# Six batches of normalised A transposed by a DMA in place of TensorE, with another token order and other scheduling constants

## The chip, the cores and the metric

The kernel runs on one core of one Trainium2 chip. The metric is device time in microseconds (us): the median of several executions, of which there are three for the kernel before. Beside them one execution was profiled; its span, from the first to the last instruction, and its own time are given below. The engines are named as in the profile: PE is TensorE, PEld its weight loads, DVE is VectorE, ACT is ScalarE, POOL is GpSimd, SP is SyncE (which only issues DMAs here).

## The reference

A Nyström attention, followed by a multiplicative feed-forward. There are 8 batches, 8 heads, 576 tokens, 64 features a head, and 32 landmarks, each the mean of 18 successive tokens.

```python
q_lm = q.reshape(B, H, m, S // m, D).mean(axis=3)      # and k_lm alike
A  = sm(q, k_lm)          # softmax(scale * q k_lm^T): 576 x 32 a head
Bm = sm(q_lm, k_lm)       # 32 x 32
C  = sm(q_lm, k)          # 32 x 576
Z  = Bm^T / (norms);  six times  Z = 2 Z - Z Bm Z
attn = A @ Z @ C @ v
x = attn as 4608 tokens x 512 features
out = (((x @ w1) * (x @ w2)) @ w3) @ w_out             # inner width 1024, out 4608 x 512
```

## The kernel before

Four heads make a quad; two quads are a batch (quads 2b and 2b + 1 are batch b). A quad's work runs through all engines: GpSimd's DMA queue loads q and k (as fp16, tokens with heads and landmarks on the partitions), DVE transposes 32 x 32 blocks of them into Tq and Tk, POOL, ACT and DVE make the landmark means and place them in lmT, PE makes the scores. Two batches are a group. A group's Bm and Z are iterated together in 32 x 32 matmuls (tile xz), Z, C and v make W (tile wT), and W is multiplied by w1 and w2 (u_mm, 64 x 32 tiles of PE) into u, 128 x 1024 a quad and matrix. So the tokens come in only at the end: the dense part computes A^T against u.

The A path of one quad, in order: `a_mm` (scores of 512 tokens in four blocks of 128, L691), `a_rest` (the last 64 tokens of both quads, odd quads only), `a_max`, `a_sub` (DVE), `a_exp` (ACT), `a_sum` (DVE), `a_norm` (POOL, L744; writes ah, of which there are two), `a_trans` (PE, L753; four transposes 128 x 128 to PSUM, a fifth in odd quads for the rest), `a_copy` (ACT, L763, and L766 for the rest; writes aT and puts tokens into their order). In a block of `a_mm`, a row of PSUM is a token (r, l): r counts within a landmark's 18 tokens, l is the landmark; block i holds four r and all 32 l. `a_copy` turns that to (l, r).

The dense part: for each batch, three thirds th of 192 tokens and eight blocks j of 128 inner columns, a task d (`d1_mm`: four matmuls of 192 columns, both products x @ w1 and x @ w2 in one PSUM bank), e (`d1_a`, L1097: ACT takes one product out to asb), f (`d1_b`, L1103: DVE multiplies the two into ab). Then, for each of 36 tiles t of 128 tokens, g (`d2_mm`: two halves of four matmuls of 512 columns, ab against w34 = w3 @ w_out), h (`d2_a`, L1129: ACT takes it out, four buffers osb) and st (`d2_store`, L1144, from SP; the last two tiles use ACT's queue as well). Tile 35 is made in two halves of 256 columns. w34 itself is computed in the first 80 us (`w34_mm`, in two fp16 parts).

The order of all instructions is not written by hand. Every piece of work is a task with an engine, an assumed duration, what it depends on, what buffers it takes and frees, and a priority (a time; the smaller goes first). `Plan.run` simulates the engines and the DMA queues with these assumptions and gives the order in which the tasks are emitted; each engine then executes its instructions strictly in that order. Among the tasks of PE that could start within 0.05 us of the first, the one of least priority wins; a task that keeps the present mode of PE (full array, or a kind of tiles) has a bonus, MP for the full mode and MT for the tiled ones. Where the priorities come from: `dense(b) = T0 + PER * b` is a batch's dense time; task d of batch b, third th, block j has `dense(b) + PER * (8 * th + j) / 24`, tile t has `T0 + PER * (128 * t + 128) / S + GO`; `att(n)` gives the quads, `lane(g)` the groups. PSUM has six banks that these tasks share (ring "P") and a wide one for the scores.

Of the kernel before, what the change touches and what calls it, by code (L numbers as in the profile page):

```python
# [15 lines left out]
S = 576  # L16
# [3 lines left out]
GRP = S // M  # L20
# [2 lines left out]
DF = 1024  # L23
HALF = 288
MP = 1.8
MT = 6.0
MY = 0.0
GR = int(2.0)
THIRD = 192
# [184 lines left out]
def kernel(  # L214
# [11 lines left out]
    nc = tc.nc  # L226
    P = Plan()
# [62 lines left out]
    def at(key, i=0):  # L290
        return P.slot[key][i]
# [3 lines left out]
    def mm(out_, lhsT, rhs, start=True, stop=True, pos=None):  # L295
        nc.tensor.matmul(out_, lhsT, rhs, start=start, stop=stop,  # L296
                         **({} if pos is None else {"tile_position": pos}))
# [4 lines left out]
    NS = [2 * len(bs) for bs in GROUPS]  # L302


    T0 = 65.0
    PER = 20.0

    def dense(b):
        return T0 + PER * b
# [1 line left out]
    def att(n):  # L311
        bs = GROUPS[GOF[n // 2][0]]
        k = n - 2 * bs[0] - 2 * len(bs) + 4
        first = dense(bs[0]) - 55.0 + 8.0 * k
        if n < 4:
            first = 10.0 + 6.5 * n
        return max(12.0 + 6.0 * n, first)

    def lane(g):
# [6 lines left out]
    LQ = int(1.0)  # L326
    NT = 2 * int(2.0)
    NE = int(2.0)
    L0 = 3.0
    UO = 2.0  # L330
    GO = 10.0


    def const_a():
# [134 lines left out]
        return fn  # L469

    W1 = 2.0
    JS = int(4.0)
    JH = 3.0
    PWL = [(), (3,), (1, 4), (1, 3, 5), (1, 3, 5, 7)][int(2.0)]
    PEB = int(2.0)
# [209 lines left out]
    def a_bank(n):  # L685
        return psS.rearrange("p a x -> p (a x)") if n % 2 else bank(at(f"pA{n}"))

    def a_cols(n):
        return 640 if n % 2 else 512

    def a_mm(n):  # L691
        def fn():
            T, lm, ps, o = Tqs[at(f"Tq{n}")], lmTs[at(f"lmT{n}")], a_bank(n), 4 if n % 2 else 2
            for i in range(4):
                for e in range(2):
                    mm(ps[:, 128 * i:128 * i + 128], T[:, o + 4 * i:o + 4 * i + 4, :, e], lm[:, 4:8, :, e],
                       start=(e == 0), stop=(e == 1))
        return fn

# [41 lines left out]
    def a_norm(n):  # L741
        def fn():
            g = a_cols(n) // M
            nc.gpsimd.tensor_tensor(  # L744
                out=ahs[at(f"ah{n}")][:, 0:g, :], in0=eas[at(f"ea{n}")][:, 0:g, :],
                in1=tinies[at(f"ta{n}")][:, 0:g].unsqueeze(2).to_broadcast([128, g, M]), op=ALU.mult)
        return fn

    def a_trans(n):
        def fn():  # L750
            ps = bank(at(f"pT{n}")).bitcast(FP16)
            for i in range(a_cols(n) // 128):
                nc.tensor.transpose(  # L753
                    out=ps[:, 128 * i:128 * i + 128],
                    in_=ahs[at(f"ah{n}")][:, 4 * i:4 * i + 4, :].rearrange("p g m -> p (g m)"),
                    identity=ident16[:, :])
        return fn

    def a_copy(n):
        def fn():  # L760
            b, qd = divmod(n, 2)
            ps, t = bank(at(f"pT{n}")).bitcast(FP16), aTs[at(f"aT{b}")]
            nc.scalar.copy(out=t[:, qd, 0:512].rearrange("p (i l r) -> p i l r", i=4, r=4),  # L763
                           in_=ps[:, 0:512].rearrange("p (i r l) -> p i l r", i=4, r=4))
            if qd:
                nc.scalar.copy(out=t[:, :, 512:S].rearrange("p a (l r) -> p a l r", r=2),  # L766
                               in_=ps[:, 512:640].rearrange("p (a r l) -> p a l r", a=2, r=2))
        return fn

    def quad_tasks(n):  # L770
# [56 lines left out]
        else:  # L827
# [7 lines left out]
            rel=[f"pA{n}"], prio=p + 0.7)  # L835
        add(f"ae{n}", "ACT", 0.63 if qd else 0.53, a_exp(n), deps=[f"as{n}"], prio=p + 3.0)
        add(f"au{n}", "DVE", 1.03 if qd else 0.9, a_sum(n), deps=[f"ae{n}"], prio=p + 4.0)
        add(f"an{n}", "POOL", 1.3 if qd else 1.05, a_norm(n), deps=[f"au{n}"], acq=[("ah", f"ah{n}", 1, 1)],
            rel=[f"ea{n}", f"ta{n}"], prio=p + 5.0)
        add(f"tA{n}", "PE", 0.36 if qd else 0.29, a_trans(n), deps=[f"an{n}", "cd"],  # L840
            acq=[("P", f"pT{n}", 1, 1)], rel=[f"ah{n}"], prio=p + 9.0, mode="full")
        add(f"aT{n}", "ACT", 0.65 if qd else 0.48, a_copy(n), deps=[f"tA{n}"] + ([f"aT{n - 1}"] if qd else []),
            acq=[] if qd else [("aT", f"aT{b}", 1, 24)], rel=[f"pT{n}"], prio=p + 9.5)


    def cv_mm(b):
# [286 lines left out]
    def d2_store(t, f0=0, f1=DM, part=None, eng=nc.sync):  # L1133
        def fn():
            k = 0
            o_sb = osb[at(f"os{t}")]
            p0 = 0
            while p0 < 128:
                b, x = divmod(128 * t + p0, S)
                i, u = divmod(x, 128)  # L1140
                n = 4 if i < 4 else 2
                w = min(128 - p0, 32 * n - u)
                if part in (None, k):
                    eng.dma_start(  # L1144
                        out=out[S * b:S * b + S, :].rearrange("(l r) f -> l r f", r=GRP)[
                            u // n:(u + w) // n, 4 * i:4 * i + n, f0:f1],
                        in_=o_sb[p0:p0 + w, f0:f1])
                p0, k = p0 + w, k + 1
        return fn

# [3 lines left out]
    def dense_tasks():  # L1154
        for k in range(3 * B):
            b, th = divmod(k, 3)
            for j in range(8):
                p = dense(b) + PER * (8 * th + j) / 24.0
                deps = [f"aT{2 * b}", f"aT{2 * b + 1}"]
                deps += [f"uo{b}{wi}{j // 4}{qd}" for wi in range(2) for qd in range(2)]  # L1160
                add(f"d{b}{j}{th}", "PE", 0.33, d1_mm(b, j, th), deps=deps + ["wo7"],
                    acq=[("P", f"pD{b}{j}{th}", 1, 1)],
                    rel=[f"u{b}0", f"u{b}1", f"aT{b}"], prio=p, mode="full")
                add(f"e{b}{j}{th}", "ACT", 0.21, d1_a(b, j, th), deps=[f"d{b}{j}{th}"],
                    acq=[("asb", f"as{b}{j}{th}", 1, 1)], prio=p)
                acq = [(f"ab{k % NCH}", f"ab{k}", 1, 2 * len(chunk_tiles(k)))] if j == 0 else []
                add(f"f{b}{j}{th}", "DVE", 0.27, d1_b(b, j, th),
                    deps=[f"e{b}{j}{th}"] + ([f"f{b}0{th}"] if j else []), acq=acq,
                    rel=[f"as{b}{j}{th}", f"pD{b}{j}{th}"], prio=p)
        for t in range(36):  # L1170
            ks = [k for k in range(3 * B) if t in chunk_tiles(k)]
            p = T0 + PER * (128 * t + 128) / S + GO
            fs = [f"f{k // 3}{j}{k % 3}" for k in ks for j in range(8)]
            if t == 35:
                for h in range(2):
                    add(f"g{t}_{h}", "PE", 0.86, d2_last(t, h), deps=fs + ([f"g{t}_0"] if h else []),
                        acq=[("P", f"pE{t}{h}", 1, 1)], rel=[f"ab{k}" for k in ks], prio=p + 0.9 * h, mode="full")
                    add(f"h{t}_{h}", "ACT", 0.3, d2_lasta(t, h), deps=[f"g{t}_{h}"],
                        acq=[] if h else [("osb", f"os{t}", 1, 4)], rel=[f"pE{t}{h}"], prio=p + 2.0)
                    for i, (eng, q) in enumerate((("SP", nc.sync), ("ACT", nc.scalar))):  # L1180
                        add(f"st{t}_{h}{i}", eng, 0.55, d2_store(t, 256 * h, 256 * h + 256, i, q),
                            deps=[f"h{t}_{h}"], rel=[f"os{t}"], prio=p + 2.0, move=0.25, lat=1.5, share=2.0)
                continue
            for h in range(2):
                add(f"g{t}_{h}", "PE", 0.86, d2_mm(t, h), deps=fs + ([f"g{t}_0"] if h else []),
                    acq=[] if h else [("P", f"pE{t}", 1, 1)], rel=[f"ab{k}" for k in ks], prio=p + 0.9 * h,
                    mode="full")
            add(f"h{t}", "ACT", 0.48, d2_a(t), deps=[f"g{t}_1"],
                acq=[("osb", f"os{t}", 1, 2 if t == 34 else 1)], rel=[f"pE{t}"], prio=p + 2.0)
            if t == 34:  # L1190
                for i, (eng, q) in enumerate((("SP", nc.sync), ("ACT", nc.scalar))):
                    add(f"st{t}_{i}", eng, 0.55, d2_store(t, 0, DM, i, q), deps=[f"h{t}"], rel=[f"os{t}"],
                        prio=p + 2.0, move=0.4, lat=1.5, share=2.0)
                continue
            add(f"st{t}", "SP", 0.85, d2_store(t), deps=[f"h{t}"], rel=[f"os{t}"],
                prio=p + 2.0, move=0.8, lat=1.5, share=2.0)
# [8 lines left out]
    for s in range(2):  # L1205
        for qd in range(2):
            for wi in range(2):
                add(f"lw{s}{qd}{wi}", "POOL", 0.62, load_w12(s, qd, wi), prio=T0 - 10.0 + 4.0 * s + wi,
                    after=T0 - 10.0 - 4.0 + 4.0 * s, move=1.6, lat=1.83, share=5.3)
    for n in range(NQ):  # L1210
        quad_tasks(n)
    for b in range(B):
# [52 lines left out]
```

## Time and profile before

| what | value |
|---|---|
| median of 3 runs | 271.1 us (269.78 to 271.92) |
| profiled execution, its own time | 271.5 us |
| its span | 269.7 us |
| mean granted clock of TensorE | 0.999 |
| busy: PE, ACT, DVE, POOL | 255.3, 191.9, 188.8, 151.1 us |
| transposes at L753 (PE) | 72 matmuls, 219 ns mean from start to end |
| copies into aT (ACT): L763, L766 | 16 of 603 ns, 8 of 297 ns |
| product at L744 (POOL) | 16 of 1160 ns mean |
| matmuls with aT and u (d) | 768 of 192 columns |
| matmuls with ab and w (g) | 280 of 512 columns, 16 of 256 |
| stores of out | 37 DMAs of 128 KB, 16 of 256 KB on SP's queue, and five smaller or on ACT's |

Matmuls are pipelined: a matmul's duration in the profile is longer than the step from its start to the next one's, so what it costs is read from the starts. A wait is told with the engine and line that waited, and the line that released it; "issue" means that nothing in the profile is seen to release it. The helper that issues matmuls is line 296 for all of them, so they are told apart by their tiles (aT, ab, xz and so on).

### The profile page before, as it was taken

How to read it: one execution, taken by the hardware profiler on the slowest of the kernel's cores; microseconds unless marked ns; L12 is line 12 of the kernel's file. 1: busy time of each engine (PE TensorE's matmuls, PEld its weight loads, DVE VectorE, ACT ScalarE, POOL GpSimd, SP SyncE). 2: the span in 40 equal slices, each digit the busy share in tenths (PEclk: the TensorE clock that was granted, in tenths of full speed). 3: DMA queues.
4: the chain of work that ended last, by engine and by line, in shares of the span. 5: the costliest groups of instructions: out<-in, count | busy, mean ns of one | idle time of the engine just before them, and what ended most of it. 6: DMA issues, size and time to landing. Idle time of an engine off the chain costs nothing.

```text
span 269.7 us, 9632 instructions
## 1 busy us (share of the span) xinstructions
PE 255.3 (95%) x3848; PEld 165.7 (61%) x3848; DVE 188.8 (70%) x519; ACT 191.9 (71%) x558; POOL 151.1 (56%) x199
## 2 busy tenths in 40 slices
PE   3998899999999989999999999999999999999993
PEld 3663455654547746666577577666766765765762
DVE  2489999899796989489779976866953561641530
ACT  3656957467589769568978798788677548659651
POOL 8427959799989996978989957711080000000000
PEclk9999999999999999999999999999999999999999
DMA  7999999999995494998797948512351121222123
GB/s 228 258 256 251 245 261 212 270 263 235 193 216 120 122 205 84 257 267 264 160 183 195 262 145 270 132 61 78 126 141 46 41 80 39 80 78 81 43 79 117
DMA packets 29518, 44.80 MB, mean 166 GB/s; under 512 B 4129, under 2 KB 18081, under 8 KB 29473
## 3 DMA queue, kind: packets, MB, share of 16 engines
q0 software_dynamic: 9568, 19.01, 34.3%
q1 hardware_dynamic: 19664, 24.91, 31.5%
q8 instruction: 30, 0.49, 0.8%
q10 hardware_dynamic: 240, 0.26, 0.3%
q14 instruction: 16, 0.12, 0.2%
HBM read 42.34 MB, written 13.37 MB: 207 GB/s over the span
## 4 chain that ended last, share of the span: by engine, by line
PE 82%; ACT 8%; DVE 5%; issue 2%; POOL 1%; ACTq 0%; DVEq 0%; POOLq 0%
PE bank L296 75%; PE wide L296 5%; ACT u L1014 3%; DVE wo L399 2%; PE bank L753 1%; ACT ec L637 1%; ACT asb L1097 1%; ACT lmT L603 1%; ACT osb L1129 1%; ACT w L467 1%; PE wide L645 1%; DVE tiny L622 1%; DVE Tq L558 1%; ACT aT L763 0%; DVE Tk L558 0%
## 5 line engine op out<-in xcount | busy, mean ns | idle before, releaser
L296 PEld LDWEIGHTS <-u 128*128 128x128 f16 x960 | 80.6, 98 | 35.1 <-issue 7.4
L1103 DVE TENSOR_TENSOR ab<-asb,bank 128x192 f16<-128x192 f16 x192 | 58.8, 346 | 37.0 <-ACT asb L1097 36.5
L296 PE MATMUL bank<-aT,u 128*128 128x192 f16 x768 | 77.2, 246 | 0.8 <-DVE ab L1103 0.3
L296 PE MATMUL bank<-w,ab 128*128 128x512 f16 (+1 forms) x296 | 73.1, 374 | 0.0
L1097 ACT CAST asb<-bank 128x192 f16<-128x192 f32 x192 | 56.0, 338 | 16.5 <-PE bank L296 15.8
L296 PE MATMUL bank<-wo,u 128*128 128x512 f16 x192 | 48.2, 380 | 2.3 <-DVE wo L399 1.3
L573 POOL TENSOR_TENSOR ls<-ls 128x128 f32<-128x128 f32 (+2 forms) x56 | 41.6, 742 | 3.6
L296 PEld LDWEIGHTS <-ab 128*128 128x128 f16 x296 | 26.6, 98 | 22.2 <-issue 3.9
L1014 ACT CAST u<-bank 128x512 f16<-128x512 f32 x64 | 34.4, 604 | 3.8 <-PE bank L296 3.6
L566 POOL TENSOR_TENSOR ls<-nat 128x1152 f32<-128x1152 f16 x14 | 33.3, 2376 | 4.9 <-ACT lm L580 3.6
L744 POOL TENSOR_TENSOR ah<-ea,tiny 128x512 f16<-128x512 f32 (+1 forms) x16 | 18.5, 1160 | 23.5 <-DVE tiny L738 8.7
L1129 ACT ACTIVATE osb<-bank 128x512 f32<-128x512 f32 x35 | 21.4, 610 | 13.5 <-PE bank L296 11.6
L680 POOL DMA_DIRECT2D ecT<-edr x48 | 26.4, 562 | 0.8 <-PE bank L296 0.7
L603 ACT COPY lmT<-lmu 32x128 f16<-32x128 f16 x64 | 18.8, 294 | 5.0 <-DVE lmu L594 3.4
L296 PE MATMUL bank<-w,wT 64*32 64x512 f16 x512 | 19.0, 380 | 0.9 <-issue 0.9
L296 PEld LDWEIGHTS bank<-xz 32*32 32x32 f32 x768 | 11.2, 105 | 8.9 <-issue 3.5
L296 PE MATMUL bank<-xz 32*32 32x64 f32 (+1 forms) x768 | 15.1, 213 | 1.0 <-issue 0.6
L450 DVE SCALAR_TENSOR_TENSOR u<-bank,u 128x512 f16<-128x512 f32 (+2 forms) x17 | 10.6, 644 | 6.2 <-ACT u L444 6.2
L622 DVE TENSOR_REDUCE tiny<-wide 128x1 f32<-128x576 f32 x16 | 12.0, 752 | 3.3 <-PE wide L296 2.7
L444 ACT ACTIVATE u<-bank 128x512 f16<-128x512 f32 (+2 forms) x17 | 9.6, 573 | 5.1 <-PE bank L296 5.1
L296 PEld LDWEIGHTS <-Tq 128*128 128x128 f16 x160 | 10.6, 97 | 4.1 <-issue 0.2
L558 DVE STREAM_TRANSPOSE Tk<-nat 128x448 f32<-128x448 f32 (+1 forms) x32 | 13.0, 443 | 0.0
(100 smaller groups left out, 322.9 us busy)
## 6 DMA issues: line engine op xcount, KB each, us to landing
vb<-in_v_dram SPq DMA_DIRECT2D x32, 160.0 KB, 6.5
out_dram<-osb SPq DMA_DIRECT2D x37, 128.0 KB, 2.3
nat<-in_k_dram POOLq DMA_DIRECT2D x16, 288.0 KB, 5.9
nat<-in_q_dram POOLq DMA_DIRECT2D x16, 288.0 KB, 7.6
vb<-in_v_dram SPq DMA_DIRECT2D x32, 128.0 KB, 6.7
out_dram<-osb SPq DMA_DIRECT2D x16, 256.0 KB, 2.9
edr<-ecx POOLq DMA_DIRECT2D x6, 640.0 KB, 4.9
w3n<-in_moe_w_dram SPq DMA_DIRECT2D x16, 128.0 KB, 7.5
```

The lines of the kernel that those rows point to most:

```text
L296: nc.tensor.matmul(out_, lhsT, rhs, start=start, stop=stop, **({} if pos is None else {"tile_position": pos}))
L558: nc.vector.transpose(out=T[:, to:to + r1 - r0].rearrange("p r l e -> p (r l e)").bitcast(FP32), in_=nats[at(f"nat{n}")][:, t, r0:r1].rear ...
L566: nc.gpsimd.tensor_tensor(out=l, in0=nat[:, :, 0:9, :], in1=nat[:, :, 9:18, :], op=ALU.add)
L573: nc.gpsimd.tensor_tensor(out=l[:, :, x:x + m, :], in0=l[:, :, x:x + m, :], in1=l[:, :, y:y + m, :], op=ALU.add)
L603: nc.scalar.copy(out=lm[r, :, h, :], in_=u[r].rearrange("p t l e -> p t (l e)"))
L622: nc.vector.reduce_max(out=mx[:, 0:1], in_=s_cols(), axis=AX.X)
L680: (nc.gpsimd if LQ else nc.sync).dma_start(out=ecTall[32 * x:32 * x + 32, i + q_, :, 0:w, :].rearrange("p h c l -> p h (c l)"), in_=src[:, ...
L744: nc.gpsimd.tensor_tensor(out=ahs[at(f"ah{n}")][:, 0:g, :], in0=eas[at(f"ea{n}")][:, 0:g, :], in1=tinies[at(f"ta{n}")][:, 0:g].unsqueeze(2 ...
L1014: nc.scalar.copy(out=uu[at(f"u{b}{qd}")][:, wi, 512 * half:512 * half + 512], in_=bank(at(f"pU{b}{wi}{half}{qd}")))
L1097: nc.scalar.copy(out=asb[at(f"as{b}{j}{th}")], in_=bank(at(f"pD{b}{j}{th}"))[:, 0:THIRD])
L1103: nc.vector.tensor_mul(ab[:, j, c0:c0 + THIRD], asb[at(f"as{b}{j}{th}")], bank(at(f"pD{b}{j}{th}"))[:, THIRD:2 * THIRD])
L1129: nc.scalar.activation(out=osb[at(f"os{t}")], in_=bank(at(f"pE{t}")), func=AXF.Copy, scale=2.0 ** -12)
```

## The change

For batches 2 to 7 (`NA` = 2), three things change together. `a_mm` takes other tokens into a block: block i holds those tokens whose landmark is i modulo 4, in the order (r, u) with r below 16 and landmark 4u + i; its weights, a view of Tq, are read with a step of 8 elements (before 2). The transposes of these four blocks leave PE, and the copy of them leaves ACT; in their place SP issues one transposing DMA a quad, which reads ah, 128 x 512 in fp16, and writes aT, 128 x 512 (task tx, 12 of them). The rest of odd quads (one transpose and one small copy) stays as it was. `d2_store` finds the rows of the changed tokens in out by their new order. The buffer ah is freed when the DMA has landed (in odd quads when the transpose of the rest has ended as well), and d of these batches waits for both DMAs.

Besides, the constants from which the priorities come are changed: MT, T0, PER, GO, JS (how many blocks of w3 have their high and low parts as separate tasks), the start of the first four quads, and the spacing of the w1 and w2 loads.

```diff
-MT = 6.0
+MT = 9.0
...
-    T0 = 65.0
-    PER = 20.0
+    T0 = 63.0
+    PER = 20.5
...
-            first = 10.0 + 6.5 * n
+            first = 12.0 + 6.5 * n
...
+    NA = int(2.0)
...
-    GO = 10.0
+    GO = 4.0
...
-    JS = int(4.0)
+    JS = int(3.0)
...
             T, lm, ps, o = Tqs[at(f"Tq{n}")], lmTs[at(f"lmT{n}")], a_bank(n), 4 if n % 2 else 2
+            by = T[:, o:o + 16].rearrange("p (i r) l e -> p i (r l) e", i=4)
+            if n // 2 >= NA:
+                by = T[:, o:o + 16].rearrange("p r (u i) e -> p i (r u) e", i=4)
             for i in range(4):
                 for e in range(2):
-                    mm(ps[:, 128 * i:128 * i + 128], T[:, o + 4 * i:o + 4 * i + 4, :, e], lm[:, 4:8, :, e],
+                    mm(ps[:, 128 * i:128 * i + 128], by[:, i, :, e], lm[:, 4:8, :, e],
                        start=(e == 0), stop=(e == 1))
...
+    def a_move(n):
+        def fn():
+            b, qd = divmod(n, 2)
+            nc.sync.dma_start_transpose(
+                out=aTs[at(f"aT{b}")][:, qd, 0:512].rearrange("p (i m) -> p i m", i=4),
+                in_=ahs[at(f"ah{n}")][:, 0:16, :].rearrange("p g m -> p (g m)"))
+        return fn
...
-            for i in range(a_cols(n) // 128):
+            for i in range(4 if n // 2 >= NA else 0, a_cols(n) // 128):
...
-            nc.scalar.copy(out=t[:, qd, 0:512].rearrange("p (i l r) -> p i l r", i=4, r=4),
-                           in_=ps[:, 0:512].rearrange("p (i r l) -> p i l r", i=4, r=4))
+            if b < NA:
+                nc.scalar.copy(out=t[:, qd, 0:512].rearrange("p (i l r) -> p i l r", i=4, r=4),
+                               in_=ps[:, 0:512].rearrange("p (i r l) -> p i l r", i=4, r=4))
...
+        if b >= NA:
+            add(f"tx{n}", "SP", 1.33, a_move(n), deps=[f"an{n}"] + ([f"tx{n - 1}"] if qd else []),
+                acq=[] if qd else [("aT", f"aT{b}", 1, 24)], rel=[f"ah{n}"], prio=p + 9.0, move=0.75, lat=1.9, share=0.5)
+            if qd:
+                add(f"tA{n}", "PE", 0.07, a_trans(n), deps=[f"an{n}", "cd"], acq=[("P", f"pT{n}", 1, 1)],
+                    rel=[f"ah{n}"], prio=p + 9.0, mode="full")
+                add(f"aT{n}", "ACT", 0.18, a_copy(n), deps=[f"tA{n}", f"tx{n - 1}"], rel=[f"pT{n}"], prio=p + 9.5)
...
+                rows = out[S * b:S * b + S, :]
+                if i < 4 and b >= NA:
+                    rows = rows.rearrange("(u i r) f -> i r u f", u=8, i=4)[i, u // 8:(u + w) // 8, :, f0:f1]
+                else:
+                    rows = rows.rearrange("(l r) f -> l r f", r=GRP)[u // n:(u + w) // n, 4 * i:4 * i + n, f0:f1]
...
-                deps = [f"aT{2 * b}", f"aT{2 * b + 1}"]
+                deps = [f"aT{2 * b + 1}"] + ([f"aT{2 * b}"] if b < NA else [f"tx{2 * b}", f"tx{2 * b + 1}"])
...
-                add(f"lw{s}{qd}{wi}", "POOL", 0.62, load_w12(s, qd, wi), prio=T0 - 10.0 + 4.0 * s + wi,
-                    after=T0 - 10.0 - 4.0 + 4.0 * s, move=1.6, lat=1.83, share=5.3)
+                add(f"lw{s}{qd}{wi}", "POOL", 0.62, load_w12(s, qd, wi), prio=T0 - 10.0 + 5.0 * s + wi,
+                    after=T0 - 10.0 - 4.0 + 5.0 * s, move=1.6, lat=1.83, share=5.3)
```

More of the change, by code (lines that the diff above doesn't have):

```diff
@@ L837, in quad_tasks @@
         add(f"au{n}", "DVE", 1.03 if qd else 0.9, a_sum(n), deps=[f"ae{n}"], prio=p + 4.0)
-        add(f"an{n}", "POOL", 1.3 if qd else 1.05, a_norm(n), deps=[f"au{n}"], acq=[("ah", f"ah{n}", 1, 1)],
+        add(f"an{n}", "POOL", 1.3 if qd else 1.05, a_norm(n), deps=[f"au{n}"], acq=[("ah", f"ah{n}", 1, 2 if qd and b >= NA else 1)],
             rel=[f"ea{n}", f"ta{n}"], prio=p + 5.0)
[L840 to L843, printed above, removed]
+        if b >= NA:
[6 more added lines that the diff above has]
+        else:
+            add(f"tA{n}", "PE", 0.36 if qd else 0.29, a_trans(n), deps=[f"an{n}", "cd"],
+                acq=[("P", f"pT{n}", 1, 1)], rel=[f"ah{n}"], prio=p + 9.0, mode="full")
+            add(f"aT{n}", "ACT", 0.65 if qd else 0.48, a_copy(n), deps=[f"tA{n}"] + ([f"aT{n - 1}"] if qd else []),
+                acq=[] if qd else [("aT", f"aT{b}", 1, 24)], rel=[f"pT{n}"], prio=p + 9.5)
     def cv_mm(b):
@@ L1142, in fn @@
                 w = min(128 - p0, 32 * n - u)
+                rows = out[S * b:S * b + S, :]
+                if i < 4 and b >= NA:
+                    rows = rows.rearrange("(u i r) f -> i r u f", u=8, i=4)[i, u // 8:(u + w) // 8, :, f0:f1]
+                else:
+                    rows = rows.rearrange("(l r) f -> l r f", r=GRP)[u // n:(u + w) // n, 4 * i:4 * i + n, f0:f1]
                 if part in (None, k):
[L1144 to L1147, printed above, removed]
+                    eng.dma_start(out=rows, in_=o_sb[p0:p0 + w, f0:f1])
                 p0, k = p0 + w, k + 1
```

## The prediction, made before the result was known

> **What bounds the kernel now.** I read the page first, then busy time by stretches of 10 us, the waits of TensorE, and the order of work on TensorE, at the places that the change touches.
>
> ```profile
> span 269.7 us, 9632 instructions
> ...
> PE 255.3 (95%) x3848; PEld 165.7 (61%) x3848; DVE 188.8 (70%) x519; ACT 191.9 (71%) x558; POOL 151.1 (56%) x199
> ```
>
> TensorE (PE) is busy for 255.3 of 269.7 us; no other engine is over 71%. The remaining 14.4 us are: 4.5 before its first matmul, 4.4 after its last (it ends at 265.3), 5.1 of gaps that the waits name, and 0.4 in pieces too small to be listed. The waits of TensorE, complete, say what ended them (line, releaser: us, times, longest):
>
> ```profile
> PE bank L296 <- issue: 1.5, 2, 0.9
> PE bank L296 <- DVE wo L399: 1.3, 2, 0.7
> PE bank L296 <- ACT u L444: 1.0, 1, 1.0
> PE bank L296 <- DVE ab L1103: 0.6, 2, 0.4
> PE wide L645 <- ACT ec L637: 0.4, 1, 0.4
> PE bank L296 <- ACT w L467: 0.2, 1, 0.2
> PE bank L296 <- ACT aT L766: 0.2, 1, 0.2
> ```
>
> The order of time places them: 2.63 us between 24 and 31 (wo, u, ec), 2.48 between 81 and 138, none from 138 to 265.3. A microsecond of TensorE work removed after 138 is thus one off the end, and before that nearly so. What the removed transposes cost is read from the order of TensorE's work around quads 14 and 15 (start, us from first start to last end, xcount):
>
> ```profile
> 190.78 0.39 PE L296 MATMUL wide<-lmT,Tq 128*128 128x128 f16 x4
> 191.02 0.38 PE L753 MATMUL bank<-ident,ah 128*128 128x128 f16 x4
> 191.24 0.82 PE L296 MATMUL bank<-aT,u 128*128 128x192 f16 x8
> ...
> 197.46 0.44 PE L753 MATMUL bank<-ident,ah 128*128 128x128 f16 x5
> 197.74 1.03 PE L296 MATMUL bank<-w,ab 128*128 128x512 f16 x4
> ```
>
> The second column overlaps the next row; the steps between starts are what TensorE pays: 191.24 - 191.02 = 0.22 us for four, 0.28 for five, 55 ns each. The last lines that I use are those of the end:
>
> ```profile
> 255.55 1.81 PE L296 MATMUL bank<-aT,u 128*128 128x192 f16 x20
> 257.20 1.03 PE L296 MATMUL bank<-w,ab 128*128 128x512 f16 x4
> 258.06 0.49 PE L296 MATMUL bank<-aT,u 128*128 128x192 f16 x4
> 258.39 1.03 PE L296 MATMUL bank<-w,ab 128*128 128x512 f16 x4
> 259.25 0.82 PE L296 MATMUL bank<-aT,u 128*128 128x192 f16 x8
> 259.92 5.36 PE L296 MATMUL bank<-w,ab 128*128 128x512 f16 x32
> 260.30 0.62 DVE L1103 TENSOR_TENSOR ab<-asb,bank 128x192 f16<-128x192 f16 x2 [1.00 <-ACT asb L1097]
> ```
>
> (One task d is 4 of the aT,u matmuls; one half of an output tile is 4 of w,ab; the DVE line stands further down in the answer's order of time.) Under the last 32 matmuls, which begin with tile 33, VectorE finishes the last product that tiles 34 and 35 need, at 260.92.
>
> **The change part by part.**
>
> Transposes. Quads 4 to 15 lose four each: 12 x 0.22 = 2.64 us of TensorE, all between 71.6 (quad 4) and 197.7. Odd quads keep one. Taken: -2.64; it could be 12 x 0.23 = 2.76 by the longest step. [...]
>
> Copies. ScalarE (ACT) loses 12 of the copies at L763, 603 ns mean: 7.2 us of 191.9. ScalarE is not the bound; of TensorE's gaps after 71 us, 0.34 name it (w 0.18, aT 0.16). Taken: -0.34; the ends are 0 and -2.48 (all gaps of that stretch close).
>
> The transposing DMAs. No transposing DMA is in the trace. Each moves 128 x 512 fp16, 128 KB. Landing: a store of 128 KB takes 2.3 us, a v load of that size 6.7, the slowest row (w, 256 KB) 9.0; I bound it by 2.3 and 9.0. What covers it: matmuls with aT, counted by stretches, 96 a batch, reach batch 2 at about 129 us, 3 at 150, 4 at 180, 5 at 200, 6 at 225, 7 at 240, while the aT of those batches is written by 81, 101, 133, 150, 182 and 199. The least slack is 41 us, so at either end it costs nothing; nothing in the trace speaks for a gain either. If that cover were gone, each batch would pay the landing, up to 6 x 9 = 54 us. The ah buffer (two of them) is held from the product on POOL until the DMA lands, and the next quad but one, which wants it, is some 23 us later on average (126 us for 11 intervals); in the closest run (quads 4 to 6, transposed at 71.6, 80.5 and 86.6) 15.0 us. Nothing.
>
> SP's queue. Twelve more issues; an issue of a store shows 0.55 us when alone, the diff's planner assumes 1.33: 7 to 16 us between 71 and 200, on a queue that waits 94.5 us for ScalarE alone. Each waits for POOL's product, and behind it stand output stores and v loads. A store held back keeps one of four output buffers; tiles come about every 4 to 5 us, and a store lands in 2.3 to 2.9, so the three that are left cover a wait of 3 x 4 - 2.9 = 9 us. POOL's own order gets no new instruction. Nothing, with the rival below.
>
> A scores by every fourth token. The same 8 matmuls; their weights are now read with a step of 8 elements in place of 2. The loads from Tq with step 2 show 97 ns, those of u with step 1 show 98, and the matmuls start every 57 ns either way: the load hides under its neighbours. Taken 0, as the step that the trace shows costs nothing; the upper end is 96 loads no longer overlapped, 96 x (97 - 57) = 3.8 us. Less than nothing is excluded: the matmuls already run at 57 ns.
>
> Stores of the changed tokens. The same 2 KB rows in another order. Only the last tile's is on the path: 64 KB lands in 2.1 us and 128 KB in 2.3. Taken 0, ends 0 and +0.2. [...]
>
> The new order. GO falls from 10 to 4, T0 to 63, PER rises to 20.5. In the stretch from 220 us TensorE follows the priorities strictly: d(7,j,2) has T0 + PER(7 + (16+j)/24), tile t has T0 + PER(128t+128)/576 + GO. Before, d0 to d7 have 218.3 to 224.2, the halves of tile 32 221.7 and 222.6, tile 33 226.1: five d, half a tile, one d, half, two d, then tile 33, which is what the lines above show. After, d0 to d7 have 220.2 to 226.1 and tile 33's halves 221.9 and 222.8. So they run after d2 and d3, and four d come last with nothing behind them but tiles 34 and 35, which need the last product. From the lines: TensorE is done issuing d7 at 259.92, VectorE's product ends at 260.92, and a semaphore follows; the bubble is 1.0 to 1.1 us, up to 1.6 if the 0.60 us output copy of tile 33 stands ahead of the last casts on ScalarE. Taken: +1.05; ends 0 (some other work left) and +1.65.
>
> The rest of the order. For quads 0 to 3 att rises by 0, 0.5, 1 and 1.5, and w3's fourth block has no separate high half to fill with (JS 3). This meets the 2.63 us of gaps at 24 to 31: ends -2.6 (all closed) and +2.6 (doubled); taken 0, for later quads help the weights on VectorE and ScalarE and the lost filler harms. MT 9 holds a tiled mode longer. A change of mode costs some 0.1 us: four w,ab matmuls step 0.87 before the same mode and 0.96 before a tiled one. I count 128 changes. Ends 0 and -1.0 (ten fewer); taken 0, as steps of one chain wait for VectorE and can't be joined.
>
> Sum, against the profiled execution's own time of 271.5 (span 269.7 and 1.8 around it): 271.5 - 2.64 - 0.34 + 1.05 = 269.6. That execution stands 0.4 above the median of the runs, 271.1; so 269.2 in the median's terms, 0.7% less.
>
> **The rivals** (all in the median's terms).
>
> B, the order gains as well: no bubble at the end and most gaps closed. 269.2 - 1.05 - 2.1 (rest of the 2.48) = 266.0. For it: ScalarE was busy for 9.85 of 10 us in 80 to 90, where early output tiles ask less of it than d tasks. Against: 1.5 of the 2.48 have no releaser in the profile ("issue"), which no order addresses.
>
> C, the gain is eaten: the gaps at 24 to 31 double, or the bubble has its upper size. 269.2 + 2.6 = 271.8, no change. For it: these gaps wait for VectorE, which is 9.9 of 10 us busy in 30 to 40. Against: the priorities there shift by 1.5 us at most.
>
> D, the strided weight loads are no longer hidden: 269.2 + 3.8 = 273.0, still within 1%. Against: the loads at step 2 cost what contiguous ones do.
>
> E, slower: transposing DMAs so slow that they become the bound. Place: the ah buffers and SP's queue. Twelve of them have 126 us plus 41 of slack, 14 us each; from there it decides. At 16 us each: 12 x 16 - 167 = 25 us, 294. Against: the slowest landing is 9.0. For: these are 2-byte elements moved across partitions, a kind of transfer that no row shows.
>
> **How the numbers follow.** A measurement here can tell about 1% from no change, 2.7 us: faster is below 268.4, slower above 273.8. Chances: forecast 0.52 (its own range 267.8 to 270.6, a quarter of it under 268.4), B 0.24, C 0.13, D 0.05, E 0.06. Faster: 0.13 + 0.24 = 0.37. Slower: E 0.06, and 0.05 from the upper ends of C and D: 0.11. The same: 0.52. The range reaches from B, 266.0, to C with a little of D, 272.6, and leaves out E, half of D, and B's lower end.
>
> **What would show it.** Transposes at L753 24 in place of 72, copies of 128x512 into aT 4 in place of 16; TensorE busy about 252.7. Weight loads from Tq still 97 ns and matmuls every 57 ns. A gap of about 1 us on TensorE behind the last aT,u matmul, released by VectorE's ab. Transposing DMAs landing in under 9 us, and no wait of TensorE or ScalarE that names them. Wrong would be: gaps on TensorE elsewhere between 30 and 260 of over 3 us in sum, a product on POOL that waits for ah, output copies that wait for stores, or a TensorE that ends before the last store for longer than 4.4 us.

## The result, and the profile after

The changed kernel takes 281.4 us (median of 4 runs, 279.96 to 284.5) where the kernel before takes 271.5 beside it (269.78 to 272.76): a ratio of 1.035, 95% interval 1.027 to 1.043. It is 3.5% slower. The forecast was 269.2, within 1%, with 0.11 on slower. The profiled execution took 281.4 us, 9.9 more than that of before. Executions more than 1.5% above the fastest of their kernel are left out of every ratio here and below; of e6_scratch, e10_go and e11_planned it is such an execution that was profiled, so these three profiles are read for places and not for sizes.

The head of the page after, against the lines shown of before:

```profile
span 279.4 us, 9550 instructions
...
PE 253.1 (91%) x3800; PEld 164.3 (59%) x3800; DVE 186.9 (67%) x519; ACT 185.7 (66%) x546; POOL 151.6 (54%) x199
...
DMA packets 35844, 46.37 MB, mean 166 GB/s; under 512 B 10456, under 2 KB 24408, under 8 KB 35800
```

TensorE lost 2.2 us of work, as meant, and ScalarE 6.2, yet the span grew by 9.7. What the engines do takes no longer in sum: they wait more. The third line shows what was added: 6,327 packets of under 512 B (4,129 before). Twelve transposing DMAs of 128 KB in packets of 256 B are 12 x 512 = 6,144 of them.

The waits of TensorE after (its wait for `osb<-in_moe_w_dram` is mostly, with 4.6 us, the one ahead of its first matmul, which before stands as 4.5 at another releaser):

```profile
PE bank L296 <- ACT aT L779: 8.5, 3, 6.9
PE bank L296 <- DMA osb<-in_moe_w_dram: 5.3, 2, 4.6
PE bank L296 <- DMA nat<-in_q_dram: 1.6, 1, 1.6
...
PE bank L296 <- DMA ecT<-edr: 1.1, 1, 1.1
```

The first line is new and the largest: TensorE waits for L779, ScalarE's small copy of both quads' last 64 tokens, three times, once for 6.9 us. Before, the same copy (L766) cost 0.2. The order of time shows how so small an instruction stops the core (rows chosen from SP, PE and ACT; in brackets the idle time ahead and its releaser):

```profile
97.64 2.29 SPq L756 DMA_TRANSPOSE aT<-ah  x1
...
99.20 0.22 PE L765 MATMUL bank<-ident,ah 128*128 128x128 f16 x1
...
107.56 0.27 ACT L779 COPY aT<-bank 128x128 f16<-128x128 f16 x1 [7.68 <-DMA aT<-ah]
107.72 0.32 ACT L1118 CAST asb<-bank 128x192 f16<-128x192 f32 x1
...
107.88 1.86 PE L296 MATMUL bank<-w,ab 128*128 128x512 f16 x4 [6.93 <-ACT aT L779]
```

At 97.64 SP issues the transposing DMA of quad 7. TensorE's transpose of the rest is done at 99.4, but the copy behind it waits until 107.56 for that DMA. ScalarE took its instructions in the order of the program: the next cast, which needs nothing of the DMA, started at 107.72, behind the copy, and TensorE, whose banks these free, at 107.88. Busy time by stretches of 10 us shows what it costs beyond the wait (PE, PEld, DVE, ACT and POOL busy, granted clock, DMA share, GB/s):

```profile
90.00:100.00 10.00, 9.98 (x166) 7.09 (x168) 8.78 (x27) 5.82 (x18) 9.11 (x12) 1.00 0.91 183
100.00:110.00 10.00, 3.07 (x64) 1.05 (x64) 2.53 (x11) 1.47 (x4) 5.95 (x10) 0.69 1.15 142
110.00:120.00 10.00, 9.98 (x274) 7.20 (x259) 4.55 (x14) 8.03 (x27) 4.96 (x5) 0.97 0.70 175
```

TensorE is busy for 3.07 of 10 us, and the clock granted to it falls to 0.69 in this stretch: the four w,ab matmuls behind the gap took 1.86 us where four take 1.03 elsewhere. The same view in finer stretches has 1.00 from 101.0 to 103.7, when TensorE already stands idle, 0.50 from 103.8 to 110.5 and 1.00 from 110.6 to 120. TensorE's 2.60 us of work from 107.9 to 110.5 would, by an estimate from these, have taken 1.3 less at 1.00.

Why did 128 KB take 10 us? The DMA view of 97 to 108 us (40 slices of 0.275 us; the digits are the busy share of the 16 DMA engines, the second line what they moved):

```profile
DMA  4998999999899999000000000009999894979996
GB/s 77 218 218 159 226 185 218 176 209 201 223 388 483 278 326 109 17 8 17 17 8 16 31 17 24 34 21 175 125 86 127 77 232 112 267 149 290 350 432 194
...
ecT<-edr POOLq DMA_DIRECT2D x4, 80.0 KB, 8.4
```

The digits count a packet where it starts: for 3 us (slices 17 to 27) hardly any starts, and 8 to 34 GB/s pass, though q and k loads are in the queues. In the packets' record, 23 packets that began between 101.1 and 101.4 are open all this time and end at 104.45 or later. Eighteen of them are 256 B packets of the transposing DMA, whose median is 18 ns; these eighteen take 3.1 to 3.4 us each and end within 0.1 us of one another. Beside them packets of loads and stores pass one at a time, the first nine of 2,304 B, most of them 173 ns from start to start. What the eighteen waited for is not shown, as the record doesn't name a packet's engine; that it was the DMA engine with the longest backlog is the author's guess. The transposing DMA's first packets start at 100.7 us, its last end at 106.0. The small moves of ecT that were issued among these took 8.4 us to land; over the whole run they take 5.1 and 4.4 us (80 and 64 KB), 3.2 and 2.8 before.

Where no loads were queued, the same DMA was quick, 2.9 us from its issue to the copy behind it (order of time around quad 15):

```profile
212.11 1.27 SPq L756 DMA_TRANSPOSE aT<-ah  x1
...
215.05 0.27 ACT L779 COPY aT<-bank 128x128 f16<-128x128 f16 x1 [0.73 <-DMA aT<-ah]
```

The end, where the prediction placed a bubble of 1.05 us:

```profile
269.54 1.15 PE L296 MATMUL bank<-aT,u 128*128 128x192 f16 x12
...
270.53 3.64 PE L296 MATMUL bank<-w,ab 128*128 128x512 f16 x24
270.58 0.88 DVE L1124 TENSOR_TENSOR ab<-asb,bank 128x192 f16<-128x192 f16 x3 [1.00 <-ACT asb L1118]
...
274.30 2.10 ACTq L1170 DMA_DIRECT2D out_dram<-osb  x2
```

No bubble: the last tiles start behind the last d without a gap. Behind the last matmul 5.2 us pass where 4.4 passed before; two issues on ScalarE's queue take 2.10 us, which before took 1.45:

```profile
265.39 1.45 ACTq L1144 DMA_DIRECT2D out_dram<-osb  x2
```

### The profile page after: what moved, and what is told of

The parts are those of the page before. It is cut to its first block, busy times and chain, and to the rows that moved or that the text cites. A ratio compares the mean times of both kernels' runs of the same rounds, so it can differ in the third digit from the quotient of the medians.

```text
span 279.4 us, 9550 instructions
## 1 busy us (share of the span) xinstructions
PE 253.1 (91%) x3800; PEld 164.3 (59%) x3800; DVE 186.9 (67%) x519; ACT 185.7 (66%) x546; POOL 151.6 (54%) x199
## 4 chain that ended last, share of the span: by engine, by line
PE 62%; DMA 15%; DVE 7%; ACT 7%; POOL 5%; issue 3%; ACTq 0%; SPq 0%; POOLq 0%
PE bank L296 57%; DMA nat<-in_q_dram 7%; DMA aT<-ah 5%; PE wide L296 3%; DMA ecT<-edr 3%; DVE ab L1124 2%; ACT u L1035 2%; POOL ah L748 1%; DVE wo L400 1%; ACT ec L638 1%; POOL ls L574 1%; ACT w L468 1%; ACT lmT L604 1%; DVE tiny L720 1%; DVE tiny L623 1%
## 5 line engine op out<-in xcount | busy, mean ns | idle before, releaser
L296 PE MATMUL bank<-aT,u 128*128 128x192 f16 x768 | 76.3, 246 | 2.2 <-ACT aT L779 1.5
L1118 ACT CAST asb<-bank 128x192 f16<-128x192 f32 x192 | 55.0, 335 | 17.9 <-PE bank L296 16.2
L1035 ACT CAST u<-bank 128x512 f16<-128x512 f32 x64 | 33.5, 600 | 3.9 <-PE bank L296 3.6
L623 DVE TENSOR_REDUCE tiny<-wide 128x1 f32<-128x576 f32 x16 | 11.9, 742 | 5.7 <-ACT bsc L630 5.3
L559 DVE STREAM_TRANSPOSE Tq<-nat 128x576 f32<-128x576 f32 (+2 forms) x24 | 12.6, 552 | 2.9 <-DMA nat<-in_q_dram 2.8
L296 PE MATMUL bank<-vb,ecT 128*32 128x64 f32 x640 | 12.1, 221 | 1.5 <-DMA ecT<-edr 1.1
```

The source lines that it names most:

```text
L296: nc.tensor.matmul(out_, lhsT, rhs, start=start, stop=stop, **({} if pos is None else {"tile_position": pos}))
L559: nc.vector.transpose(out=T[:, to:to + r1 - r0].rearrange("p r l e -> p (r l e)").bitcast(FP32), in_=nats[at(f"nat{n}")][:, t, r0:r1].rear ...
L623: nc.vector.reduce_max(out=mx[:, 0:1], in_=s_cols(), axis=AX.X)
L1035: nc.scalar.copy(out=uu[at(f"u{b}{qd}")][:, wi, 512 * half:512 * half + 512], in_=bank(at(f"pU{b}{wi}{half}{qd}")))
L1118: nc.scalar.copy(out=asb[at(f"as{b}{j}{th}")], in_=bank(at(f"pD{b}{j}{th}"))[:, 0:THIRD])
```

## The experiments

Three theories stand at the start. W, the wait: the copy L779 writes both quads' last 64 tokens in one instruction, `t[:, :, 512:S]`. Its write runs, as a span of addresses, across the second quad's first 512 tokens, which that quad's own DMA writes; so it waits for that DMA, where the planner was told of the DMA of the quad before it (`tx{n-1}`). In the list of instructions of the changed kernel the copy waits for the DMA queue counter that quad 7's transposing DMA raises, DMAHW7 (the brackets show what each waits for; the DMA itself waits for the counter's earlier use):

```
SP  L756 DmaTransposeAnt aT_100<-ah_96 128x4x128 [waits DMAHW7_49,Pool_49]
ACT L779 TensorCopy aT_100<-bank_61 128x2x64 [waits DMAHW7_49,PE_49]
```

O, the order: the loss comes from the new constants. C, the crowd: the 6,144 small packets hold up the other transfers. Out of C came later, on record with e9_plain, L, the lockstep: a transposing DMA among loads stops the other transfers as well, whoever waits for it. All ratios are to the kernel before, run beside them on the same chip, with 95% intervals; differences between runs are differences of ratios.

The planner plans anew for each kernel, so most runs differ in their order as well. By the sequences of tiles in the traces, TensorE's order is the same in five pairs: before and b0_again, after and e2, e3 and e4, e1 and e5, e6 and e9. Their differences are the clean ones. Between after and e1 at least 628 of 3,800 matmuls stand in another order, between after and e11 at least 452.

| run | what is different | ratio | interval |
|---|---|---|---|
| after | the change | 1.035 | 1.027 to 1.043 |
| e1_order | new constants alone | 1.013 | 1.007 to 1.019 |
| e2_split | change, L779 in two copies | 1.021 | 1.007 to 1.036 |
| e3_oldorder | change, constants of before | 1.054 | 1.043 to 1.065 |
| e4_oldsplit | e3 with two copies | 1.029 | 1.016 to 1.042 |
| b0_again | the kernel before | 1.002 | 0.996 to 1.007 |
| e5_tokens | e1 and token order, stores | 1.015 | 1.009 to 1.022 |
| e6_scratch | e1 and 12 unused transposing DMAs | 1.031 | 1.021 to 1.040 |
| e7_last | e2, batch 7 as before | 1.017 | 1.008 to 1.026 |
| e9_plain | e6 with plain DMAs | 1.014 | 1.007 to 1.021 |
| e8_late | two copies, batches 6 and 7 only, constants of before | 1.005 | 1.001 to 1.010 |
| e10_go | of the new constants only GO and MT | 1.011 | 1.007 to 1.015 |
| e11_planned | change, planner told of the wait | 1.012 | 1.002 to 1.021 |

**e1_order**: the new constants without any DMA.

```diff
-    NA = int(2.0)
+    NA = int(8.0)
```

> All batches as in the kernel before (transposes on TensorE, no transposing DMA, old token order), with the new scheduling constants alone. Theory W (the loss is ScalarE's copy of the rest, L779, which waits for the odd quad's own transposing DMA, and TensorE behind it): 270 to 274 us, since no such wait is left and only some 2 to 3 us of gaps ahead of 60 us may stay. Rival O (the new constants make the loss): 277 us or more. Rival C (the 6144 packets of 256 bytes crowd the other transfers): as W.

Measured: 275.1 us, between W's range and O's, and 1.3% slower; profiled execution 274.3 us. So the new constants by themselves cost about a third of the loss, though in an order that isn't quite the change's. The waits of TensorE behind the first matmul come to 7.8 us where 5.2 stood before, none longer than 1.0 us; none is the bubble, as its last d, too, is followed by the last tiles with no gap.

**e2_split**: the copy in two instructions, one a quad, so that neither crosses the region of a DMA.

```diff
-nc.scalar.copy(out=t[:, :, 512:S].rearrange("p a (l r) -> p a l r", r=2),
-               in_=ps[:, 512:640].rearrange("p (a r l) -> p a l r", a=2, r=2))
+for a in range(2):
+    nc.scalar.copy(out=t[:, a, 512:S].rearrange("p (l r) -> p l r", r=2),
+                   in_=ps[:, 512 + 64 * a:576 + 64 * a].rearrange("p (r l) -> p l r", r=2))
```

> The changed kernel; the copy of the rest is made as two copies of 64 columns, one a quad, so that its write region no longer spans the region that the transposing DMA writes; all else and the order of tasks unchanged. W: 281.4 - 8.5 (TensorE's waits for L779) - about 1.5 (clock lost behind the long gap) = 271.4 us, 270 to 273, and no wait for the DMA at the copy. O and C: 278 us or more, the gap elsewhere.

Measured: 1.021, with 277.4 us outside W's range and just short of O's and C's. The list of instructions shows the copies waiting for TensorE alone, and the waits of TensorE have lost the line of L779:

```profile
PE bank L296 <- DMA osb<-in_moe_w_dram: 5.4, 2, 4.4
PE bank L296 <- issue: 4.2, 4, 2.0
PE bank L296 <- DVE wo L400: 1.1, 2, 0.7
```

The wait is gone as W says, and 1.4% with it, in the same order (the intervals overlap). But 2.1% are left, though no wait in the profile names a transposing DMA any more. 4.2 us now have no releaser in the profile ("issue"; 0.4 in e1). The longest of them stands ahead of the first matmuls that read ecT:

```profile
108.63 2.36 PE L296 MATMUL bank<-vb,ecT 128*32 128x64 f32 x80 [1.98 <-issue]
```

The trace's semaphore records name what ended it. TensorE's queue waits for 2.2 us, until 108.3, for the counter of an ecT move that POOL issued at 101.4 and that landed at 108.2, 6.8 us later: a move issued while quad 7's transposing DMA (97.96 to 106.0) was under way. In e7 the same wait of 2.6 us ends with a move that took 7.7 us. In e1 the eight moves of this group land in 2.1 to 3.8 us, in e9, beside plain DMAs, in 2.3 to 4.1. So the transposing DMA reaches TensorE by a second way, through the transfers that it holds up.

**e3_oldorder and e4_oldsplit**: the change with the constants of before, and the same with two copies.

> The DMA transposes and the new token order with all scheduling constants of before. W: between 270 and 282 us, according to how many of the copies of the rest meet a transposing DMA still under way; TensorE's waits that name L779 explain the distance to 269. O: 269 us. C: 278 us or more with waits that name other DMAs.

> The DMA transposes with the constants of before and the copy of the rest split in two. W: 268 us (271.5 - 2.6 of transposes, some gaps), 267 to 270, faster than before. O: 269 us. C: 275 us or more.

Measured: 1.054 and 1.029. Both miss W's ranges: e3 with 286.8 us, where W allowed 282, and e4 with 280.3, where W expected 267 to 270 and C 275 or more. In e3 the waits of TensorE begin with the same line as after:

```profile
PE bank L296 <- ACT aT L779: 7.2, 4, 3.2
```

On one chip and in one order the wait is worth 2.4%, and it doesn't come from the new constants. With the DMAs in, the new constants help (1.035 against 1.054, and 1.021 against 1.029, the intervals of the second pair overlapping), while without them they cost 1.3%: the two are not simply added.

**b0_again**: the kernel before, run as an experiment.

> The kernel before once more, for a profile on the same chip as the others of this call: ratio 1.00. It shows whether the gaps of TensorE in the first 60 us, which all four kernels of the first call have 2 to 3 us larger than the first profile of before, belong to the chip or to the change.

Measured: 1.002. Its profile has a wait of 1.7 us at 50.9 for ec that the first profile of before didn't show. Gaps of this size ahead of 60 us come with the execution, so none of them is counted to the change here.

**e5_tokens**: everything but the DMAs. The transposes and copies are as before, with the new token order in the scores and the stores.

```diff
-            for i in range(4 if n // 2 >= NA else 0, a_cols(n) // 128):
+            for i in range(a_cols(n) // 128):
...
+            else:
+                nc.scalar.copy(out=t[:, qd, 0:512], in_=ps[:, 0:512])
```

> The new constants, the new token order of batches 2 to 7 and its stores, but the transposes on TensorE and a plain copy on ScalarE as before (no transposing DMA). Theory C (what is left of the loss with the copy split comes from the transposing DMAs, which delay the other transfers and SP's queue): 1.013 as the new constants alone, up to 1.017 for a longer last store. Rival S (the strided weight loads and the scattered stores): 1.025 or more.

Measured: 1.015, 0.2% over e1. The weight loads of TensorE from Tq, in e1 first, then in e5:

```profile
L296 PEld LDWEIGHTS <-Tq 128*128 128x128 f16 x160 | 10.5, 97 | 4.4 <-issue 2.0
```

```profile
L296 PEld LDWEIGHTS <-Tq 128*128 128x128 f16 x160 | 11.8, 126 | 4.3 <-issue 2.0
```

The 96 changed loads bring the mean from 97 to 126 ns, so a load with a step of 8 takes about 97 + 29 x 160 / 96 = 145. Most of that lies beside matmuls: the loads took 96 x 48 ns = 4.6 us longer, but by steps between starts the matmuls with Tq cost only 0.6 us more in e5 than in e1, in the same order.

**e6_scratch and e9_plain**: is it the transposing, or only 12 more DMAs? e6 is e1 with one transposing DMA a quad from ah into a tile that nothing reads; aT is made as before. e9 has a plain DMA in its place, with the same 128 KB in the same 512 packets of 256 B, issued at the same place and holding ah until it lands. The two run in the same order on every engine.

```diff
-nc.sync.dma_start_transpose(
-    out=scs[at(f"sc{n}")].rearrange("p (i m) -> p i m", i=4),
-    in_=ahs[at(f"ah{n}")][:, 0:16, :].rearrange("p g m -> p (g m)"))
+nc.sync.dma_start(
+    out=scs[at(f"sc{n}")][:, :, 0:128],
+    in_=ahs[at(f"ah{n}")][:, 0:16, :].rearrange("p (i g) m -> p i (g m)", i=4))
```

> The new constants with everything as in the kernel before, and in addition twelve transposing DMAs from ah into a tile that nobody reads. C: 1.013 + 0.02 = 1.03, since the transposes on TensorE stay and the DMAs crowd. S: 1.013.

> As e6_scratch, but the twelve DMAs into the tile that nobody reads are plain copies of the same 128 KB in the same 512 pieces of 256 bytes, at the same places of SP's queue, and hold ah likewise. Theory L (a transposing DMA stops all 16 DMA engines until the one with the longest backlog has caught up): 1.013 to 1.018, as the new constants alone. Rivals P (small packets crowd the queues) and Q (SP's queue and the held ah): 1.03 as with e6_scratch.

Measured: 1.031 and 1.014, intervals that don't overlap. Twelve plain DMAs cost 0.1% over e1, twelve transposing ones 1.8%. So it is the transposing, and not the number or the size of the packets. The DMA view of 89 to 101 us, 40 slices of 0.3 us, first of e6:

```profile
DMA  9999999999799999999794999090059090829279
GB/s 161 154 184 200 169 161 108 108 123 295 235 361 351 401 332 341 223 130 97 31 50 33 67 32 124 9 32 0 0 17 53 9 48 9 40 16 68 29 134 229
...
nat<-in_k_dram POOLq DMA_DIRECT2D x1, 288.0 KB, 12.1
nat<-in_q_dram POOLq DMA_DIRECT2D x1, 288.0 KB, 13.1
out_dram<-osb SPq DMA_DIRECT2D x1, 256.0 KB, 12.1
...
sc<-ah SPq DMA_TRANSPOSE x1, 12.2
```

and of e9 at the same place in the program:

```profile
DMA  9999799999989999989989999966878493754910
GB/s 184 215 177 235 224 397 361 447 380 337 308 191 197 189 192 146 177 108 146 177 146 191 230 288 312 309 147 173 255 211 212 111 231 77 199 137 123 164 27 27
...
nat<-in_k_dram POOLq DMA_DIRECT2D x1, 288.0 KB, 5.2
nat<-in_q_dram POOLq DMA_DIRECT2D x1, 288.0 KB, 6.3
...
sc<-ah SPq DMA_DIRECT2D x1, 128.0 KB, 4.3
```

With the transposing DMA in the queues the loads of the next q and k take 12.1 and 13.1 us, with the plain one 5.2 and 6.3, and an output store 12.1 against 6.8 (the 4.6 that e9's whole answer has is the median of two). The transposing DMA itself, quad 6's, takes 12.2; quad 6's plain one was issued ahead of this view, at 87.69, and took 5.7 (the 4.3 shown is quad 7's). The traffic of e6 stays under 70 GB/s for most of 95 to 100 us, that of e9 between 77 and 312. How long the hold-up is in e6's other executions isn't known, and it is the one place of its size here: at the other eleven the two DMAs land within 1.7 us of each other, at the other loads since 70 us within 1.9, and over the whole run the median landing is nearly the same, 4.5 us against 4.1.

The packets tell the two kinds apart. None of the 6,144 packets of 256 B that e9's plain DMAs have takes longer than 66 ns. Of as many of the transposing DMAs 25 take over 1 us in the changed kernel, up to 3.4, and 34 in e2, up to 2.9. That fits L. One difference is left untried: SP's issues take 15.0 us for e6's twelve DMAs and 8.7 for e9's.

In e6 the longest wait of TensorE behind its start is for the product on POOL:

```profile
PE bank L766 <- POOL ah L749: 4.6, 1, 4.6
```

POOL didn't wait for a free ah there; it came late, behind its ecT issues, which waited for held-up transfers (first the landing of the edr move, 9.9 us where e9 has 5.3, then those of the k and q loads):

```profile
99.41 3.31 POOL L682 DMA_DIRECT2D ecT<-edr  x6 [3.25 <-issue]
104.30 0.55 POOL L682 DMA_DIRECT2D ecT<-edr  x1 [1.57 <-DMA nat<-in_k_dram]
105.86 0.55 POOL L682 DMA_DIRECT2D ecT<-edr  x1 [1.02 <-DMA nat<-in_q_dram]
106.42 1.28 POOL L749 TENSOR_TENSOR ah<-ea,tiny 128x640 f16<-128x640 f32 x1
```

By the medians of e6 and e9, 4.5 and 4.1 us, the transposing DMAs landed nearly as fast as the plain ones; not so at the one place above, with 12.2 us against 5.7, and quad 7's takes 9.8 in the changed kernel against 4.3 in e9.

**e7_last**: e2 with batch 7 as before, so that the last tiles are stored as before.

> The copy of the rest split in two as in e2_split, and batch 7 as in the kernel before, so that the last stores have the old order; batches 2 to 6 by DMA. Against 1.021 of e2_split: 0.8 us less in what follows TensorE's last matmul and 0.44 us more transposes, 1.019 to 1.021 by both theories if the stores matter only at the end; under 1.015 if S holds for the stores of batch 7.

Measured: 1.017, against 1.021 for e2 and between what the theories and S expected; the intervals overlap, the profiles are clearer. Behind the last matmul stand 4.2 us in e7 and 5.3 in e2, and the last two issues on ScalarE's queue, e2's first:

```profile
268.54 2.10 ACTq L1171 DMA_DIRECT2D out_dram<-osb  x2
```

```profile
268.38 1.45 ACTq L1171 DMA_DIRECT2D out_dram<-osb  x2
```

What differs is the store of the changed tokens: a half tile's outermost dimension has 8 rows in place of 16, and the two issues together take 0.65 us longer, on a queue with nothing left behind it to hide that.

**e8_late**: constants of before, two copies, and only batches 6 and 7 by DMA, after most of the loads (edit: `NA = int(6.0)`).

> The constants of before, the copy of the rest split in two, and only batches 6 and 7 by DMA, most of whose transposing DMAs come when no loads are under way any more. L: the DMAs cost nothing there, 16 transposes fewer are worth 16 x 0.055 = 0.9 us, the longer last stores cost 0.8: 0.997 to 1.003. If every transposing DMA costs the same wherever it stands (1.8% for twelve): 1.004 to 1.008.

Measured: 1.005 in 12 runs, interval 1.001 to 1.010. That is above L's range and inside that of the rival by which every transposing DMA costs the same wherever it stands; the interval reaches into both, so e8 speaks against L rather than for it. The four DMAs have their last packets 3.8, 3.3, 2.0 and 2.6 us after their issue; nine of their packets still take over 1 us, up to 1.9, so the lockstep is milder there and not absent. The longer last store adds 0.7 us (0.25%). That leaves some 0.6% (0.5 and the 0.3 that 16 transposes should give, less 0.25) without a cause that these runs show; the order, too, differs from that of before in at least 97 matmuls. It is not faster than before either: no version here is.

**e10_go**: e1 with only GO and MT new.

```diff
-MT = 6.0
+MT = 9.0
...
-    GO = 10.0
+    GO = 4.0
```

> No DMA transposes; of the new constants GO = 4 and MT = 9 alone, the others as before. If the loss of the new order (1.013) comes from the earlier output tiles: 1.010 to 1.015; if from the first 60 us (JS, the start of the first quads, T0): 1.00.

Measured: 1.011, so most of the new order's 1.3% comes with these two. Which waits they bring stays open: its profile has 3.7 us of waiting for ec at 52, where b0's has 1.7.

**e11_planned**: the change as it is, but the planner is told that the copy waits for `tx{n}`, and that a transposing DMA lands 9.0 us after its issue (1.9 in the change).

```diff
-    add(f"aT{n}", "ACT", 0.18, a_copy(n), deps=[f"tA{n}", f"tx{n - 1}"], ...
+    add(f"aT{n}", "ACT", 0.18, a_copy(n), deps=[f"tA{n}", f"tx{n}"], ...
```

> The changed kernel with the wait kept, but told to the planner: the copy of the rest depends on the odd quad's own transposing DMA, which lands 9 us after it is issued, so it comes later in ScalarE's order. W: as with the split copy, 1.015 to 1.025, with TensorE's waits for L779 under 2 us. If the wait's place in ScalarE's order did not matter: 1.035.

Measured: 1.012, interval 1.002 to 1.021, a little under the range expected. The copy still waits for the DMA, but L779 stands in no wait of TensorE or ScalarE any more. A wait that the planner knows can be hidden. The order of all engines has moved with it, so the run doesn't tell what the wait alone had cost: it stands 0.9% under e2, which has the same DMAs and no wait at all (the intervals overlap). By e2 1.4, by e11 up to 2.3 of the change's 3.5% thus come from a dependency that was left out of the plan.

## Why the prediction was wrong

The parts of the loss, by differences of ratios: the new order +1.3% (e1), token order and stores +0.2 (e5 less e1), transposing DMAs +1.8 (e6 less e1), transposes removed -1.0 (2.67 us). Their sum is +2.3, and e2, which has them all, measures +2.1. The wait of L779 adds 1.4 (after less e2), 3.5 in all. Each difference is uncertain by about 1%, e1 and e6 don't have the change's order, and e3, e4 and e11 show that order and DMAs depend on each other; that the sum fits is in part luck, and the split is a rough one.

*Transposes, -2.64*: right. By steps between starts they cost 4.12 us before and 1.46 after, -2.67. The profile after has 24 of them, as foreseen.

*Copies, -0.34*: ScalarE lost 6.2 us of work, but the gaps of TensorE that name it didn't close, they grew. What mattered was not ScalarE's load but its order.

*The transposing DMAs, "at either end it costs nothing"*: this is the step that failed, in two ways. First, its slack of 41 us was counted for d, the reader of aT. ScalarE's copy of the rest, which writes the same tile, was not counted as a waiter; nor was it asked, as for every added wait, what is queued behind it on its engine. ScalarE's waits that name the DMA come to 11.9 us in four copies, a sign that the prediction itself had listed. The diff itself shows that copy with a new dependency. The landing stayed near the bounds given: at the longest wait the copy was released 9.9 us after the issue (2.3 to 9.0 had been set). With the right waiter the upper bound would have told of a stop of ScalarE; it measured 8.5 us of TensorE's waits, and a granted clock of 0.50 from 103.8 to 110.5. Secondly, only the DMA's own landing was priced. What it does to the other transfers was not, and it is the larger part in e2: 1.8% by e6, where plain DMAs of the same packets cost 0.1%. No row of before could have given that price; it should have stood as an unknown with an upper end, and the range with it.

*SP's queue, nothing*: borne out by e9 for twelve issues of 8.7 us in all, which cost 0.1% over e1; the longer issues of the transposing DMAs weren't tried by themselves.

*A scores, taken 0, upper end 3.8*: mis-sized by 0.6. The loads did become slower, 145 ns in place of 97, but most of that is hidden. The inference from a step of 2 to one of 8 was wrong, the cover was right.

*Stores, taken 0, at most +0.2*: +0.8 at the very end, 0.65 of it from the issue and not from the landing.

*The end, +1.05*: 0. The step assumed that the last tiles need the last product at once; their first matmuls use blocks of ab that are done, and by the time that the last one is wanted it is there.

*The rest of the order, 0 between -2.6 and +2.6*: it measured +1.3% in e1, which with the bubble taken out is beyond the upper end (3.5 us). TensorE was 95% busy: a new order had 5 us of gaps to close and no limit on those that it adds, so the term should have leaned to a loss.

*The rivals*: E named the right object and the right doubt (a kind of transfer that no row shows), but put the place at ah and the threshold at 14 us each. The deciding place was ScalarE, where one DMA in a burst of loads, landing after 9.9 us, was enough.

What stays open: which waits GO and MT bring; what ends the other "issue" waits (2.2 of 4.2 us in e2, 3.2 of 5.5 in e7; 1.5 before); and the last 0.6% of e8. That packets of the transposing DMA stay open while others pass one at a time was seen in the packets but not tried by itself.

## What to carry to other kernels

When work goes from an engine to a DMA, list every instruction that touches the tile the DMA writes, other writers of neighbouring columns too, and look at what is queued behind each on its engine, as the casts were here behind a copy that waited 7.68 us; a copy over a strided span can wait for a transfer that writes only the gap within the span, as L779 did, and its two halves in e2 did not. Price a new kind of transfer by its effect on the traffic around it: a kernel of the same transfers in plain form, with the result unused, tells the transposing from the mere traffic (1.8% and 0.1% here). Where a planner orders the work, compare kernels that came out in the same order. And where TensorE is 95% busy, 48 transposes at 55 ns are 2.7 us at most, a gain that one badly placed wait takes back three times over.

## What was not expected of the hardware

A transposing DMA of 128 x 512 fp16 has its last packet 2.0 to 8.5 us after its issue in the changed kernel, a plain DMA of the same packets 2.0 to 8.1 in e9: the transposing one isn't much slower itself. But its 256 B packets, 18 ns in the median, can stay open for 3.4 us while loads are queued, and for about 3 us the other packets then passed one at a time; the plain one's took 66 ns at most. SP's issue of it takes 1.2 to 2.3 us, a plain store's 0.55. The two last issues on ScalarE's queue take 0.65 us longer where a half tile's store has 8 rows in its outermost dimension and not 16. And a weight load with a step of 8 elements takes about 145 ns, by an estimate from the means of e1 and e5, where steps of 1 and 2 take 98 and 97.
